# Attention and two expert layers on one core: sums in halves of banks, a second bank for the first products, idle products, and y stored by another queue

## The chip, the cores and the metric

The kernel runs on one core of one Trainium2 chip. A time is the device time of one execution in microseconds (us). Its parts are TensorE (PE, matrix products; its weight loads are listed as PEld), VectorE (DVE), ScalarE (ACT), GpSimd (POOL) and SyncE (SP); transfers are issued by SP's queue and by ACT's queue and are moved by 16 DMA engines.

## The reference

Three stages, one after the other, all in float32 at the interface:

```
state = alpha[t] * state + k[t] v[t]^T ;  y[t] = q[t] state     # 4 batches, 8 heads, 768 steps, head size 48
x = y as 3072 tokens x 384
out = sum over e of p[:, e] * (relu(x @ w1[e]) @ w2[e])         # 4 experts, 384 -> 1024 -> 384, p normalised
h = out @ w_in ; result = (h * clip(h + 3, 0, 6) / 6) @ w_out   # 384 -> 2048 -> 384; w_in, w_out arrive as float64
```

## The kernel before

**Attention** is done in 12 pieces of 256 time steps (n = 0 to 11; class `Attention`). A piece is a tree: products of q, k and alpha on DVE (`p0` to `p3`, `u0`, `u1`, `kk`, `kq`, `tp`), transposes on PE (`T_tp`, `T_k0` ... `T_q1`, copied out by ACT), four levels of score products (`Sc` copies by ACT, `C` products on PE, `Su` updates on DVE, level 0 to 3), `M` masks, `K` and `U` for the state, `Y`, `L` and `ST` summing y in two banks of PSUM, and `Z` for the running state. `A` copies y out of PSUM (tiles `ys0`, `ys1`, ACT) and stores it to DRAM (`x_d`) in four transfers; `R` loads it back with tokens in the order the expert layer wants (`rx`), and `XS` splits it into a high and a low part (`xh` on ACT, `xl` on DVE). `load_vt` fetches v again for `U` (`vt`) and for the four levels of `L` (`vl`, eight transfers).

**The expert layers** work on 6 blocks of 512 tokens, block 0 in two halves of 256. A step takes 128 hidden units: `mm1` (nine products into one bank `ph`), ACT makes `hh = relu(ph)`, DVE makes the rest `hl` from `ph` and `hh`, and `mm2` adds nine products (three for each of the three 128-row pieces m) into the sums `po`. In program order `mm2` of a step stands behind `mm1` of the next one. A run of steps with one expert is a visit; when it ends, `finish` multiplies the three sums by the expert's weights on DVE (`t`, `pb`), and they are stored to DRAM (`acc_d`). Phase 0 does the first 7 slices of 256 hidden units (14 steps) for each block or half block, phase 1 the other experts, phase 2 the last layer.

The order on each engine is written out by hand. Piece 0 of attention and the start of piece 1 stand ahead of the first step (the `u(...)` calls); after that, groups of pieces 1 to 11 are put between the steps of phase 0 (`group`, `rest`, the tables GROUP, BETWEEN and CHUNK): two pieces to a half of block 0, two to each later block. Every engine takes its instructions in this order, and each of SP's and ACT's transfers waits on one of eight counters, DMAHW0 to DMAHW7, which the transfers of both queues take in turn; a transfer waits for the one that had its counter before.

PSUM has eight banks: four for attention (`psa`), one for `ph` (`ps1`), three for `po` (`ps2`).

Of the kernel before, what the change touches and what calls it, by code (L numbers as in the profile page):

```python
# [21 lines left out]
class Attention:  # L22
# [268 lines left out]
    def tree(self, n):  # L291
# [24 lines left out]
        def T(src, tag, half):  # L316
            if half == 0:
                s[tag] = wk(tag, [P, 2, NP, P])
            pt = self.ps(f"p{tag}{half}_{n}")
            for i in range(4):  # L320
                pe.transpose(pt[:, P * i : P * i + P], src[:, 4 * half + i].rearrange("p h d -> p (h d)"), self.ident)  # L321
            out = s[tag].rearrange("p j r (c i) -> p j i c r", i=8)[:, :, 4 * half : 4 * half + 4]
            src_ = pt.rearrange("p (i j c r) -> p j i c r", i=4, j=2, r=NP)
            for j in range(2):
                nc.scalar.copy(out[:, j], src_[:, j])

# [158 lines left out]
        def A():  # L485
            for j in range(2):
                ys = wk(f"ys{j}", [P, NP, P])
                nc.scalar.copy(ys, s["py"][j])
                for h in range(2):
                    nc.scalar.dma_start(  # L490
                        self.y_d.rearrange("(r h e) t -> h e r t", r=NP, h=2)[h][:, :, n * U + P * j : n * U + P * j + P],
                        ys[64 * h : 64 * h + D],
                    )
# [45 lines left out]
def tile_gla__then__moe__then__moe2(  # L539
# [52 lines left out]
    ps1 = ctx.enter_context(tc.tile_pool(name="ps1", bufs=1, space=PSUM))  # L592
    ps2 = ctx.enter_context(tc.tile_pool(name="ps2", bufs=3, space=PSUM))
    psa = ctx.enter_context(tc.tile_pool(name="psa", bufs=4, space=PSUM))

    three = const.tile([P, 1], F32, name="three")
# [174 lines left out]
    def mm1(vi, f):  # L771
# [6 lines left out]
        cs = slice(vv["lo"], vv["lo"] + n)  # L778
        other = late and (vv["kind"] == 2 or f % 2)
        ph = (psa if other else ps1).tile([P, 512], F32, tag="psa" if other else "ps1", name=f"ph_{vi}_{f}")  # L780
        fs = slice(z * P, z * P + P)
# [29 lines left out]
    def mm2(vi, f):  # L811
# [6 lines left out]
        nt = KT if vv["kind"] == 1 else n // P  # L818
        if first:
            second = vv["phase"] == 1 and vi % 2  # L820
            pools = [(psa, "psa") if second else (ps2, "ps2") if m < 3 else (ps1, "ps1") for m in range(nt)]
            accs[vi] = [pool.tile([P, 512], F32, tag=tag, name=f"po_{vi}_{m}") for m, (pool, tag) in enumerate(pools)]
        for m in range(nt):
            ms = slice(m * P, m * P + P)
            for o, (w, h) in enumerate(((wh, hh), (wl, hh), (wh, hl))):
                fl = dict(start=(first and o == 0), stop=(last and o == 2))
                if vv["kind"] == 1:
                    pe.matmul(accs[vi][m][:, 0:n], w[:, z, ms], h[:, 0:n], **fl)  # L828
                else:
                    pe.matmul(accs[vi][m][:, 0:DM], h[:, ms], w[:, z, :], **fl)  # L830
            if last:
                finish(vi, m)

# [25 lines left out]
    def finish(vi, m):  # L859
# [4 lines left out]
        if vv["kind"] == 1:  # L864
# [6 lines left out]
            if vv["phase"] == 0:  # L871
                after(1, lambda: nc.sync.dma_start(acc_d[vv["e"]][:, m, t0 : t0 + n], t[:, 0:n]))
                return
# [26 lines left out]
    def u(names, n=0):  # L900
        at.run(n, names)
# [3 lines left out]

    u("p0 p1 p2 u0 u1 cp kk kq tp T_tp T_k0 T_k1 T_q0 T_q1 p3 r0")
    at.load(1, "qka")
# [3 lines left out]
    load_w(1, 2)  # L911
    u("tls Sc0 C0 Su0 Sc1 r1 y0 C1 Su1 Sc2 y1 M0 Su2 Sc3 r2 C2 Su3 C3")
    sw(0, 0)
    u("y2 M2 K0 K1 y3 y4 y5 U Y L0 L1 L2 L3 X Z0 Z1 Z2 Z3 ST")
    at.load(1, "v")
# [154 lines left out]
```

## Time and profile before

| | us |
|---|---|
| median of 3 runs (lowest to highest) | 1458.64 (1457.69 to 1460.36) |
| the profiled execution | 1465.24 |
| its span in the trace | 1463.4 |
| PE busy, DVE busy, ACT busy | 1379.1, 839.8, 464.1 |

The profiled execution is the one that the rows below come from. A row of the timeline gives the start, the length, engine, line, what is written and read, the shape, and in brackets how long the engine had been idle before it and what ended that. Of the 40 slices of the page each stands for 36.6 us; the first 14 or so hold phase 0 with attention.

### The profile page before, as it was taken

The numbers are of one execution on the slowest core, as the hardware profiler recorded it, in microseconds if no ns is written. First come the engines' busy times: TensorE is split into PE (matmuls) and PEld (weight loads), VectorE is DVE, ScalarE is ACT, GpSimd is POOL, SyncE is SP. The second block draws the span as 40 slices with busy tenths as digits, with TensorE's granted clock in tenths as the row PEclk, the third lists the DMA queues.
The fourth block names the chain that finished last, engine by engine and source line by source line (L and its number), as shares of the span: only waits on it lengthen the run. The fifth ranks groups of instructions, "written<-read, shape, count | busy, mean of one in ns | idle before, by whom it ended". The sixth has DMA issues, their size and how long they took to land.

```text
span 1463.4 us, 25889 instructions
## 1 busy us (share of the span) xinstructions
PE 1379.1 (94%) x10772; PEld 1178.0 (80%) x10772; DVE 839.8 (57%) x1505; ACT 464.1 (32%) x843; POOL 91.5 (6%) x125
## 2 busy tenths in 40 slices
PE   4588889999999999999999999999999999999998
PEld 4477878777877787888888888888889989998997
DVE  7877866766658527875757576725543333333332
ACT  3544443333333313311111111113333333333333
POOL 2000000000000001221212121200000000000000
PEclk9788999999999999999999999999999999999999
DMA  7454442434323226632424242314201010101000
GB/s 207 139 146 135 124 132 67 135 96 136 105 81 105 84 62 216 213 123 73 133 72 133 72 133 73 119 38 125 93 26 44 1 44 0 44 1 44 1 22 22
DMA packets 127748, 132.32 MB, mean 90 GB/s; under 512 B 33680, under 2 KB 109456, under 8 KB 127632
## 3 DMA queue, kind: packets, MB, share of 16 engines
q1 hardware_dynamic: 117648, 125.96, 28.3%
q10 hardware_dynamic: 9984, 4.72, 1.3%
q8 instruction: 84, 1.38, 0.4%
q14 instruction: 32, 0.26, 0.1%
HBM read 100.71 MB, written 34.65 MB: 92 GB/s over the span
## 4 chain that ended last, share of the span: by engine, by line
PE 85%; DMA 6%; DVE 5%; ACT 2%; issue 1%; SPq 1%; ACTq 0%; DVEq 0%
PE ph L785 39%; PE po L828 24%; PE po L830 13%; DMA vl<-vd 4%; PE py L455 2%; PE py L476 1%; PE pa L365 1%; DMA rw<-in_moe_w_dram 1%; PE pu L401 1%; PE pk L389 1%; PE pkt L321 1%; DVE kt L353 1%; PE pqt L321 1%; DMA x_d<-ys 1%; DVE hl L796 1%
## 5 line engine op out<-in xcount | busy, mean ns | idle before, releaser
L793 ACT ACTIVATE hh<-ph 128x512 fp32r<-128x512 f32 (+1 forms) x206 | 117.2, 569 | 539.1 <-PE ph L785 539.1
L785 PE MATMUL ph<-xh,w0h 128*128 128x512 f32 (+1 forms) x906 | 262.2, 399 | 24.5 <-DVE hl L796 22.5
L796 DVE SCALAR_TENSOR_TENSOR hl<-ph,hh 128x512 fp32r<-128x512 f32 (+1 forms) x206 | 134.3, 652 | 242.1 <-ACT hh L793 241.8
L785 PE MATMUL ph<-xh,w0l 128*128 128x512 f32 (+1 forms) x906 | 252.6, 388 | 0.0
L785 PE MATMUL ph<-xl,w0h 128*128 128x512 f32 (+1 forms) x906 | 252.2, 388 | 0.0
L828 PE MATMUL po<-hh,w1h 128*128 128x512 f32 (+1 forms) x618 | 236.1, 382 | 2.7 <-DVE t L870 2.5
L828 PE MATMUL po<-hh,w1l 128*128 128x512 f32 (+1 forms) x618 | 234.5, 379 | 0.0
L828 PE MATMUL po<-hl,w1h 128*128 128x512 f32 (+1 forms) x618 | 234.1, 379 | 0.0
L785 PEld LDWEIGHTS ph<-xh,w0h 128*128 128x128 f32 x906 | 165.2, 194 | 51.4 <-DVE hl L796 25.6
L785 PEld LDWEIGHTS ph<-xh,w0l 128*128 128x128 f32 x906 | 171.0, 194 | 35.1
L785 PEld LDWEIGHTS ph<-xl,w0h 128*128 128x128 f32 x906 | 171.1, 194 | 34.7
L804 DVE SCALAR_TENSOR_TENSOR g<-g,ph 128x512 f32<-128x512 f32 x96 | 66.0, 688 | 191.1 <-ACT g L801 191.1
L828 PEld LDWEIGHTS po<-hh,w1h 128*128 128x128 f32 x618 | 119.7, 194 | 25.8 <-issue 2.3
L828 PEld LDWEIGHTS po<-hh,w1l 128*128 128x128 f32 x618 | 119.6, 194 | 21.2
L828 PEld LDWEIGHTS po<-hl,w1h 128*128 128x128 f32 x618 | 118.9, 192 | 21.4
L830 PE MATMUL po<-w1h,hh 128*128 128x384 f32 x384 | 130.1, 339 | 1.8 <-ACT hh L805 1.7
L830 PE MATMUL po<-w1h,hl 128*128 128x384 f32 x384 | 129.8, 338 | 0.2
L830 PE MATMUL po<-w1l,hh 128*128 128x384 f32 x384 | 129.0, 336 | 0.0
L801 ACT ACTIVATE g<-ph,three 128x512 f32<-128x512 f32 x96 | 66.2, 690 | 178.2 <-PE ph L785 178.2
L806 DVE SCALAR_TENSOR_TENSOR hl<-g,hh 128x512 fp32r<-128x512 f32 x96 | 66.6, 693 | 67.0 <-ACT hh L805 67.0
L805 ACT ACTIVATE hh<-g 128x512 fp32r<-128x512 f32 x96 | 60.6, 632 | 76.1 <-DVE g L804 76.1
L830 PEld LDWEIGHTS po<-w1h,hh 128*128 128x128 f32 x384 | 72.2, 188 | 7.8 <-ACT hh L805 2.5
(102 smaller groups left out, 1399.1 us busy)
## 6 DMA issues: line engine op xcount, KB each, us to landing
rx<-x_d SPq DMA_DIRECT2D x36, 384.0 KB
rw<-in_moe_w_dram SPq DMA_DIRECT2D x28, 384.0 KB
vl<-vd SPq DMA_DIRECT2D x96, 96.0 KB
pb<-p_d SPq DMA_DIRECT2D x28, 256.0 KB
raw<-in_moe_w_in_dram SPq DMA_DIRECT2D x24, 256.0 KB
raw<-in_moe_w_out_dram SPq DMA_DIRECT2D x24, 256.0 KB
acc_d<-t SPq DMA_DIRECT2D x20, 256.0 KB
rq<-in_q_dram SPq DMA_DIRECT2D x24, 192.0 KB
```

The source lines that it names most:

```text
L321: pe.transpose(pt[:, P * i : P * i + P], src[:, 4 * half + i].rearrange("p h d -> p (h d)"), self.ident)
L353: tt(zv, zv, tlv[:, :, 1 - x].unsqueeze(2).to_broadcast([P, nb, w]), op=mul)
L455: pe.matmul(s["py"][j][64 * h : 64 * h + 64, r, :].rearrange("p (b x w) -> p b x w", x=2, w=w)[:, :, 1, :], self.vl[64 * j : 64 * j + 64, ...
L785: pe.matmul(ph[:, 0:n], w[:, j, fs], x[:, j, cs], start=(o == 0 and j == 0), stop=(o == 2 and j == KT - 1),)
L793: nc.scalar.activation(hh[:, 0:n], ph[:, 0:n], AF.Relu)
L796: nc.vector.scalar_tensor_tensor(hl[:, 0:n], ph[:, 0:n], 0.0, hh[:, 0:n].bitcast(F32), op0=ALU.max, op1=sub)
L801: nc.scalar.activation(g[:, 0:n], ph[:, 0:n], AF.Relu, bias=three)
L804: nc.vector.scalar_tensor_tensor(g[:, 0:n], g[:, 0:n], 6.0, ph[:, 0:n], op0=ALU.min, op1=mul)
L805: nc.scalar.activation(hh[:, 0:n], g[:, 0:n], AF.Copy, scale=1.0 / 6.0)
L806: nc.vector.scalar_tensor_tensor(hl[:, 0:n], g[:, 0:n], 1.0 / 6.0, hh[:, 0:n].bitcast(F32), op0=mul, op1=sub)
L828: pe.matmul(accs[vi][m][:, 0:n], w[:, z, ms], h[:, 0:n], **fl)
L830: pe.matmul(accs[vi][m][:, 0:DM], h[:, ms], w[:, z, :], **fl)
```

## The change

1. The four stores of y are issued by SP's queue (`nc.sync`) in place of ACT's, at the same place of the program; the stores of `acc_d` are put off by one step more (`after(2)`).
2. In the two halves of block 0 `ph` takes two banks in turn (`ps1`, `ps3`). The three sums of 256 columns share two banks (`psh`): m = 0 and 1 are the halves of one bank, m = 2 has the other. The sums 0 and 1 are finished together. From block 1 on the pools are as before.
3. In piece 0, `qt` is copied out of PSUM by DVE in place of ACT; `tls` stands between `T_q0` and `T_q1`, and `p3 r0` behind both. The first split of weights (`sw(0, 0)`) moves from the middle of piece 0 to its end.
4. A function `busy(n)` issues n products of the identity with itself into a bank that nobody reads: 30 ahead of piece 0, 6, 5, 5 and 5 inside it, 20 behind it.

```diff
-                nc.scalar.copy(out[:, j], src_[:, j])
+                if n == 0 and tag == "qt":
+                    nc.vector.tensor_copy(out[:, j], src_[:, j])
+                else:
+                    nc.scalar.copy(out[:, j], src_[:, j])
...
-                    nc.scalar.dma_start(
+                    nc.sync.dma_start(
                         self.y_d.rearrange(...)
...
-    ps2 = ctx.enter_context(tc.tile_pool(name="ps2", bufs=3, space=PSUM))
+    psh = ps_ctx.enter_context(tc.tile_pool(name="psh", bufs=2, space=PSUM))
+    ps3 = ps_ctx.enter_context(tc.tile_pool(name="ps3", bufs=1, space=PSUM))
+    ps2 = None
...
+        elif vv["n"] < NB and f % 2:
+            pool, tag = ps3, "ps3"
...
+        half = n < NB
+        if first and half:
+            po = [psh.tile([P, 2, U], F32, tag="psh", name=f"po_{vi}_{x}") for x in range(2)]
+            accs[vi] = [po[0][:, 0], po[0][:, 1], po[1][:, 0]]
...
-                fl = dict(start=(first and o == 0), stop=(last and o == 2))
+                fl = dict(start=(first and o == 0 and not (half and m == 1)), stop=(last and o == 2))
...
-            if last:
-                finish(vi, m)
+            if last and (m > 0 or not half):
+                for x in (0, 1) if half and m == 1 else (m,):
+                    finish(vi, x)
...
-                after(1, lambda: nc.sync.dma_start(acc_d[vv["e"]][:, m, t0 : t0 + n], t[:, 0:n]))
+                after(2, lambda: nc.sync.dma_start(acc_d[vv["e"]][:, m, t0 : t0 + n], t[:, 0:n]))
...
+    def busy(n):
+
+        for _ in range(n):
+            pe.matmul(idle[:, 0:P], at.ident, at.ident, start=True, stop=True)
...
-    u("p0 p1 p2 u0 u1 cp kk kq tp T_tp T_k0 T_k1 T_q0 T_q1 p3 r0")
+    busy(30)
+    u("p0 p1 p2 u0 u1 cp kk kq tp T_tp T_k0 T_k1")
+    u("T_q0 tls T_q1")
+    busy(6)
+    u("p3 r0")
...
-    u("tls Sc0 C0 Su0 Sc1 r1 y0 C1 Su1 Sc2 y1 M0 Su2 Sc3 r2 C2 Su3 C3")
-    sw(0, 0)
-    u("y2 M2 K0 K1 y3 y4 y5 U Y L0 L1 L2 L3 X Z0 Z1 Z2 Z3 ST")
+    u("Sc0 C0 Su0 Sc1 r1")
+    busy(5)
+    u("y0 C1 Su1 Sc2 y1")
+    busy(5)
+    u("M0 Su2 Sc3 r2 C2 Su3")
+    busy(5)
+    u("C3 y2 M2 K0 K1 y3 y4 y5 U Y L0 L1 L2 L3 X Z0 Z1 Z2 Z3 ST")
+    sw(0, 0)
+    busy(20)
```

The instructions of ACT around the stores of y of piece 4 (`ys_4`), in block 1, before; `kc_5` and `qc_5` are the copies of level 0 and 1 of piece 5:

```order
L343 COPY kc_5_2972<-kt_2830 128x512 [waits Activation_49]
L343 COPY qc_5_2974<-qt_2957 128x512 [waits Activation_49]
L793 ACTIVATE hh_1_2991<-ph_1_2981 128x512 [waits DVE_49,PE_49]
L488 COPY ys_4_2995<-py_4_2737 128x512 [waits DMAHW6_49,DMAHW4_49]
L490 DMA x_d<-ys_4_2995 48x4x128 [waits DMAHW5_49,Activation_49]
L490 DMA x_d<-ys_4_2995 48x4x128 [waits DMAHW7_49]
L488 COPY ys_4_2999<-py_4_2738 128x512 [waits DMAHW3_49,DMAHW1_49]
L490 DMA x_d<-ys_4_2999 48x4x128 [waits DMAHW2_49,Activation_49]
L490 DMA x_d<-ys_4_2999 48x4x128 [waits DMAHW4_49]
L343 COPY kc_5_3049<-kt_2830 128x512 [waits DVE_49,PE_49]
L343 COPY qc_5_3051<-qt_2957 128x512 [waits DVE_49]
L793 ACTIVATE hh_2_3065<-ph_2_3055 128x512 [waits PE_49]
```

and now:

```order
L346 COPY kc_5_3043<-kt_2901 128x512 [waits Activation_49]
L346 COPY qc_5_3045<-qt_3028 128x512 [waits Activation_49]
L804 ACTIVATE hh_1_3059<-ph_1_3049 128x512 [waits DVE_49,PE_49]
L491 COPY ys_4_3063<-py_4_2808 128x512 [waits DMAHW1_49,DMAHW0_49]
L491 COPY ys_4_3067<-py_4_2809 128x512 [waits DMAHW3_49]
L346 COPY kc_5_3122<-kt_2901 128x512 [waits DVE_49,PE_49]
L346 COPY qc_5_3124<-qt_3028 128x512 [waits DVE_49]
L804 ACTIVATE hh_2_3141<-ph_2_3131 128x512 [waits PE_49]
```

The four transfers with their waits for the counters have gone from between the copies and `kc_5`.

SP's queue at the same place before, from the stores of `acc_d` to the load of x (`rx_4`):

```order
L872 DMA acc_d<-pb_2038 128x256 [waits DMAHW5_49,DVE_49]
L124 DMA rv_3007<-in_v_dram 128x1x384 [waits DMAHW6_49]
L124 DMA rv_3007<-in_v_dram 128x1x384 [waits DMAHW7_49]
L145 DMA vt<-vd_2692 128x2x384 [waits DMAHW2_49,DMAHW0_49,PE_49]
L151 DMA vl<-vd_2692 64x1x384 [waits DMAHW1_49,PE_49]
L151 DMA vl<-vd_2692 64x1x384 [waits PE_49]
L151 DMA vl<-vd_2692 64x1x384 [waits DMAHW3_49,PE_49]
L151 DMA vl<-vd_2692 64x1x384 [waits DMAHW4_49,PE_49]
L151 DMA vl<-vd_2692 64x1x384 [waits DMAHW6_49]
L151 DMA vl<-vd_2692 64x1x384 [waits DMAHW0_49]
L151 DMA vl<-vd_2692 64x1x384 [waits DMAHW1_49]
L151 DMA vl<-vd_2692 64x1x384 [waits DMAHW3_49,PE_49]
```

and now, from the load `vd` that stands ahead:

```order
L137 DMA vd_2763<-in_v_dram 2048x1x48 [waits DMAHW2_49]
L493 DMA x_d<-ys_4_3063 48x4x128 [waits DMAHW3_49,Activation_49]
L493 DMA x_d<-ys_4_3063 48x4x128 [waits DMAHW4_49]
L493 DMA x_d<-ys_4_3067 48x4x128 [waits DMAHW5_49,Activation_49]
L493 DMA x_d<-ys_4_3067 48x4x128 [waits DMAHW6_49]
L124 DMA rv_3075<-in_v_dram 128x1x384 [waits DMAHW7_49,DVE_49]
L124 DMA rv_3075<-in_v_dram 128x1x384 [waits DMAHW0_49]
L145 DMA vt<-vd_2763 128x2x384 [waits DMAHW2_49,DMAHW1_49,PE_49]
L151 DMA vl<-vd_2763 64x1x384 [waits PE_49]
L151 DMA vl<-vd_2763 64x1x384 [waits DMAHW3_49,PE_49]
L151 DMA vl<-vd_2763 64x1x384 [waits DMAHW4_49,PE_49]
L151 DMA vl<-vd_2763 64x1x384 [waits DMAHW5_49,PE_49]
```

The stores of y stand at the head, ahead of the loads of v, `vt` and `vl`; the stores of `acc_d` have moved behind `vl`. Before, the counters that the eight loads `vl` skip are those of ACT's stores of y.

PE in block 0, a step of the visit that goes with piece 2, before (`ph_2` is the third `mm1` of the visit, `hh_1` and `hl_1` belong to the step before it):

```order
L785 MATMUL ph_2_1427<-xh_0_643,w0h_1098 128x256 [waits DVE_49]
L785 MATMUL ph_2_1427<-xh_0_643,w0h_1098 128x256 x2
L785 MATMUL ph_2_1427<-xh_0_643,w0l_1099 128x256 x3
L785 MATMUL ph_2_1427<-xl_0_644,w0h_1098 128x256 x3
L828 MATMUL po_0_1390<-hh_1_1381,w1h_956 128x256 [waits Activation_49]
L828 MATMUL po_0_1390<-hh_1_1381,w1l_957 128x256
L828 MATMUL po_0_1390<-hl_1_1382,w1h_956 128x256
L828 MATMUL po_1_1391<-hh_1_1381,w1h_956 128x256
```

and now:

```order
L796 MATMUL ph_2_1500<-xh_0_718,w0h_1172 128x256 x3
L796 MATMUL ph_2_1500<-xh_0_718,w0l_1173 128x256 x3
L796 MATMUL ph_2_1500<-xl_0_719,w0h_1172 128x256 x3
L849 MATMUL po_0_1461<-hh_1_1452,w1h_1030 128x256 [waits Activation_49]
L849 MATMUL po_0_1461<-hh_1_1452,w1l_1031 128x256
L849 MATMUL po_0_1461<-hl_1_1453,w1h_1030 128x256 [waits DVE_49]
L849 MATMUL po_0_1461<-hh_1_1452,w1h_1030 128x256
L849 MATMUL po_0_1461<-hh_1_1452,w1l_1031 128x256
```

The wait for DVE has moved from the first product of `mm1` to the third product of `mm2`, and the second three products of `mm2` go to the same tile as the first.

## Rows read from the trace of the kernel before

**Rows 1.** The page: busy time of the engines, share of the span, instructions.

```profile
PE 1379.1 (94%) x10772; PEld 1178.0 (80%) x10772; DVE 839.8 (57%) x1505; ACT 464.1 (32%) x843; POOL 91.5 (6%) x125
```

**Rows 2.** The busy table by stage: up to the first step, the first half of block 0, the second half, blocks 1 to 5 of phase 0 as far as attention reaches. Columns: from:to, length, busy time and instructions of PE, PEld, DVE, ACT, POOL, granted clock, DMA share, GB/s.

```profile
0.00:49.59 49.59, 20.65 (x420) 18.23 (x420) 39.03 (x78) 20.66 (x44) 10.04 (x29) 0.92 0.62 170
49.59:126.00 76.41, 59.62 (x941) 55.37 (x942) 61.12 (x117) 33.45 (x70) 0.00 (x0) 0.80 0.50 142
126.00:205.88 79.88, 68.84 (x1263) 63.78 (x1262) 64.63 (x138) 35.88 (x83) 0.00 (x0) 0.94 0.48 134
205.88:525.80 319.92, 301.16 (x3824) 243.27 (x3823) 200.67 (x376) 116.64 (x242) 0.00 (x0) 0.95 0.34 100
```

**Rows 3.** The same table for single pieces of attention from block 1 on, cut at the transposes of q (pieces 5, 10 and 11), and the sum over all seven.

```profile
205.88:253.89 48.01, 44.25 (x554) 35.74 (x554) 27.54 (x53) 17.20 (x36) 0.00 (x0) 0.93 0.35 98
...
441.12:483.67 42.55, 41.51 (x553) 33.69 (x554) 34.68 (x67) 17.18 (x36) 0.00 (x0) 1.00 0.33 93
483.67:525.80 42.13, 40.38 (x544) 32.59 (x543) 15.52 (x27) 13.54 (x26) 0.00 (x0) 1.00 0.24 71
sum 319.92, PE 301.16 PEld 243.27 DVE 200.67 ACT 116.64 POOL 0.00; mean PE 43.02 PEld 34.75 DVE 28.67 ACT 16.66 POOL 0.00
```

**Rows 4.** Who made PE wait from 205.88 to 525.8: total, times, longest.

```profile
PE pa L365 <- ACT qc L343: 14.3, 7, 3.2
PE ph L785 <- DVE hl L796: 4.4, 7, 0.7
```

**Rows 5.** PE's timeline at two products of level 1 and the `mm1` behind them, in the second half of block 0 and in piece 10.

```profile
146.56 1.13 PE L365 MATMUL pa<-qc,kc 48*64 48x64 f32 x32 [4.68 <-ACT qc L343]
...
451.49 0.69 PE L365 MATMUL pa<-qc,kc 48*64 48x64 f32 x32 [0.29 <-ACT qc L343]
452.90 0.96 PE L785 MATMUL ph<-xh,w0h 128*128 128x512 f32 x3 [0.71 <-DVE hl L796]
```

**Rows 6.** ACT's timeline in block 1 where piece 4's y is stored.

```profile
211.93 0.59 ACT L488 COPY ys<-py 128x512 f32<-128x512 f32 x1 [1.37 <-DMA rv<-in_v_dram]
214.51 3.33 ACTq L490 DMA_DIRECT2D x_d<-ys  x2
217.94 0.62 ACT L343 COPY kc<-kt 128x512 f32<-128x512 f32 x1 [5.43 <-DMA x_d<-ys]
```

**Rows 7.** The chain that ended last, at the same place (start, length, what), and where the loads `vl` end on SP's queue.

```profile
211.72 5.79 DMA vl<-vd
...
217.54 0.31 ACTq L490
...
217.94 0.63 ACT kc L343
...
220.54 4.21 PE ph L785 x9
...
228.23 2.27 PE ph L785 x9
```

**Rows 8.** SP's timeline there (the load of v and the eight loads `vl`), and PE's timeline at the first `L` of piece 5, which reads them.

```profile
206.94 1.19 SPq L124 DMA_DIRECT2D rv<-in_v_dram  x2
...
209.74 6.17 SPq L151 DMA_DIRECT2D vl<-vd  x8
...
239.96 1.16 PE L455 MATMUL py<-asb,vl 64*64 64x64 f32 x64
```

**Rows 9.** Who made PE wait in the first and in the second half of block 0.

```profile
PE ph L785 <- DVE hl L796: 14.8, 6, 5.8
...
PE pa L365 <- ACT qc L343: 1.5, 1, 1.5
...
PE pa L365 <- ACT qc L343: 6.8, 4, 4.7
PE ph L785 <- DVE hl L796: 3.3, 5, 1.7
```

**Rows 10.** ACT's and DVE's timeline in block 0: a cast of weights, and a copy and an update of level 1.

```profile
71.22 0.83 ACT L745 CAST w1h<-rw 128x768 fp32r<-128x768 f32 x1 [6.16 <-DMA rw<-in_moe_w_dram]
...
145.37 0.62 ACT L343 COPY kc<-kt 128x512 f32<-128x512 f32 x1 [4.89 <-DMA x_d<-ys]
...
146.02 0.69 DVE L353 TENSOR_TENSOR kt<-kt,tl 128x512 f32<-128x512 f32 x1 [4.76 <-ACT kc L343]
```

**Rows 11.** POOL, PE and DVE in piece 0 and up to the first step.

```profile
2.88 0.29 POOL masks.py:199 TENSOR_SCALAR_AFFINE_SELECT ident<-ident 128x128 f32<-128x128 f32 x1
...
12.66 0.66 PE L309 MATMUL ptt<-ident,tp 128*128 128x128 f32 x2 [12.66 <-DVE tp L232]
13.11 1.92 PE L321 MATMUL pkt<-ident,kp 128*128 128x128 f32 x8
...
49.59 1.01 PE L785 MATMUL ph<-xh,w0h 128*128 128x256 f32 x3 [1.96 <-ACT xh L764]
...
18.69 0.69 DVE L353 TENSOR_TENSOR kt<-kt,tl 128x512 f32<-128x512 f32 x1 [3.48 <-ACT kc L343]
...
27.96 0.95 DVE L746 TENSOR_TENSOR w0l<-rw,w0h 128x768 fp32r<-128x768 f32 x1
```

**Rows 12.** The chain that ended last, later in block 0: a `mm1`, and eight transposes.

```profile
111.20 2.29 PE ph L785 x9
...
119.75 1.02 PE pk L389 x8
```

More of the change, by code (lines that the diff above doesn't have):

```diff
@@ L592, in tile_gla__then__moe__then__moe2 @@
     ps1 = ctx.enter_context(tc.tile_pool(name="ps1", bufs=1, space=PSUM))
-    ps2 = ctx.enter_context(tc.tile_pool(name="ps2", bufs=3, space=PSUM))
     psa = ctx.enter_context(tc.tile_pool(name="psa", bufs=4, space=PSUM))
+    ps_ctx = ExitStack()
+    psh = ps_ctx.enter_context(tc.tile_pool(name="psh", bufs=2, space=PSUM))
+    ps3 = ps_ctx.enter_context(tc.tile_pool(name="ps3", bufs=1, space=PSUM))
+    ps2 = None
     three = const.tile([P, 1], F32, name="three")
@@ L778, in mm1 @@
         cs = slice(vv["lo"], vv["lo"] + n)
-        other = late and (vv["kind"] == 2 or f % 2)
-        ph = (psa if other else ps1).tile([P, 512], F32, tag="psa" if other else "ps1", name=f"ph_{vi}_{f}")
+        pool, tag = ps1, "ps1"
+        if late and (vv["kind"] == 2 or f % 2):
+            pool, tag = psa, "psa"
+        elif vv["n"] < NB and f % 2:
+            pool, tag = ps3, "ps3"
+        ph = pool.tile([P, 512], F32, tag=tag, name=f"ph_{vi}_{f}")
         fs = slice(z * P, z * P + P)
@@ L818, in mm2 @@
         nt = KT if vv["kind"] == 1 else n // P
-        if first:
+        half = n < NB
+        if first and half:
+            po = [psh.tile([P, 2, U], F32, tag="psh", name=f"po_{vi}_{x}") for x in range(2)]
+            accs[vi] = [po[0][:, 0], po[0][:, 1], po[1][:, 0]]
+        elif first:
+            nonlocal ps2
+            if ps2 is None:
+                ps_ctx.close()
+                ps2 = ctx.enter_context(tc.tile_pool(name="ps2", bufs=3, space=PSUM, reuse_waits="tile"))
             second = vv["phase"] == 1 and vi % 2
@@ L825, in mm2 @@
             for o, (w, h) in enumerate(((wh, hh), (wl, hh), (wh, hl))):
-                fl = dict(start=(first and o == 0), stop=(last and o == 2))
+                fl = dict(start=(first and o == 0 and not (half and m == 1)), stop=(last and o == 2))
+                if half:
+                    fl["skip_group_check"] = True
                 if vv["kind"] == 1:
@@ L904, in sw @@
         split_w(y, i, nc.vector)
-    u("p0 p1 p2 u0 u1 cp kk kq tp T_tp T_k0 T_k1 T_q0 T_q1 p3 r0")
+    idle = ps1.tile([P, 512], F32, tag="ps1", name="idle")
+    def busy(n):
[6 more added lines that the diff above has]
+    u("p3 r0")
     at.load(1, "qka")
```

## The prediction

> **What bounds the kernel now.** I read the page first: PE is busy for 94% of the span [rows 1], so a gain can come only from the remaining time of PE and from stretches at the lower of its two clocks. The busy table by stage says where these are [rows 2]. After 525.8 us PE is all but full and nothing is changed there. Before it the span loses in four stages: PE is busy 20.65 of 49.59 us up to the first step, 59.62 of 76.41 in the first half of block 0, 68.84 of 79.88 in the second, 301.16 of 319.92 in the blocks behind, and the granted clock is 0.80 to 0.95 in the last three. Then the lists of waits, stage by stage, and the timeline around the longest waits.
>
> In the blocks behind (seven pieces of attention, 205.88 to 525.8) there are only two waits on PE, seven times each: for the copies of q at level 1, 14.3 us, and for `hl`, 4.4 us [rows 4]. ACT's timeline shows why: between the two copies of level 0 and of level 1 it stores y, and the copy `kc` behind the stores starts after 5.43 us of waiting for a transfer [rows 6]. The chain is plainer still: a load `vl` of SP's queue takes 5.79 us to land, then ACT issues a store in 0.31 us, then `kc` runs [rows 7]. In the order the stores wait for counters that the loads of v and `vl` had just taken, so ACT, and with it PE, waits for loads with which neither has to do. After such a wait nine products of `mm1` take 4.21 us where they take 2.27 a step later [rows 7], which is the half clock.
>
> **The stores of y.** Four transfers leave ACT at each piece. What stands behind `ys` on ACT is then the copy `kc` at once. For the blocks behind, the price is read from the pieces: piece 10 (441.12 to 483.67) shows what one costs almost without the jam, clock 1.00 and PE busy 41.51 of 42.55 us; piece 11 has 40.38 of 42.13 [rows 3]. Six at 41.51 and one at 40.38 are 289.4 us; the seven took 319.9 [rows 3], so 30.5 us are to be had. I take 28: piece 10 keeps 0.71 us of waiting for `hl` [rows 5], and about half of that in each piece may stay.
>
> What the stores cost on SP: each waits for its copy, and behind it stand the loads of v, `vt`, `vl`, then the stores of `acc_d` and the load of x. In block 1 the second copy of y, freed of the 1.37 us before it [rows 6], would end near 211.2; SP began its loads of v at 206.94, so it starts some 4 us later, and after four issues (3.33 us for two of them on ACT with its waits, 0.31 us for one without [rows 6, 7], so 1.2 to 6.7 us; I take 2.5) the loads of v start at 213.7 in place of 206.94. Everything behind moves by 6.8 us: `vl` is issued up to 222.7 in place of 215.9 [rows 8], and with the longest landing seen, 5.79, is there by 228.5. The first `L` runs at 239.96 now [rows 8] and would run 5.5 us earlier (the average of a piece's gain plus a little), at 234.5. So 6 us of cover are left in a block of 512 tokens, and I cost the move at nothing there. In block 0 a piece has half the steps to hide it; if the cover goes, PE waits at `L`, up to those few us per piece, and that is in the lower bounds below. The stores of `acc_d`, one step later and behind `vl`, free buffers that are needed a visit later; nothing.
>
> By the Trainium skill ("DMA: Bandwidth & Descriptors", section "Issuing engines are not separate DMA queues") starting transfers from several engines saves only the sequencer's time to start them, and transfers of all queues share the same engines. By that rule this part would be worth a few tenths of a microsecond per piece, since nothing about the transfers themselves changes; the row with the wait of 5.43 us speaks against applying it here, because what is waited for is not the store's own transfer. It is the second rival below.
>
> **Second half of block 0** (79.88 us). PE waits 6.8 us for the copies of q and 3.3 for `hl` [rows 9]. The longest, 4.68 us [rows 5], is the same jam: `kc` had waited 4.89 us on a store of y, and DVE's update stood idle for 4.76 [rows 10]. I take 6 of the 6.8 for the stores. The second bank lets `mm1` run while DVE still works on the `hl` of the step before, so that only `mm2` waits for it, behind another `mm1`; 2 of the 3.3. Together 8. The other end is DVE: it is busy 64.63 of the 79.88 [rows 2], so not over 15.2; the lower end is 3, if the loads behind the stores come late for `L`.
>
> **First half of block 0** (76.41 us). Here 14.8 us of waiting are put down to `hl` [rows 9], but the longest is not the bank's: ACT waited 6.16 us for weights to land before the cast at 71.22 [rows 10], and its relu stands behind that cast. Two banks let one `mm1` go ahead in such a gap, 2.29 us at the clock seen there [rows 12], twice or so, and the stores' part is the one wait of 1.5 [rows 9] with the slow products behind it. DVE is busy 61.12 [rows 2], the weights land no earlier. I take 5, bounds 0 and 15.3. That the sums of 256 columns share banks costs a wait for one more `finish` at three changes of visit, under a microsecond each; nothing.
>
> **Up to the first step** (49.59 us). The transposes at 13.11 run at half clock, 1.92 us for eight where eight take 1.02 later [rows 11, 12]. The 30 idle products can start when POOL has the identity, at 3.2 [rows 11]. No row shows one; a plain float32 product leaves two records where a transpose leaves one, so I estimate one at two transposes, 0.48 us or, at full clock, 0.26 [from rows 11, 12]. Thirty end between 10.9 and 17.6; the first transpose is ready at 12.66 [rows 11], so they cost up to 4.9 us or nothing. If the clock rises on the way, they end about when that is ready: nothing. DVE idles 3.48 us before 18.69 for ACT's copies [rows 11]; now it makes half of these copies itself (some 0.5 us each, 2 us), takes `p3 r0` behind them (1.9), and loses the split of weights (0.95, at 27.96 [rows 11]), so that it ends piece 0 up to half a microsecond earlier. Behind it PE's `Y`, `L` and `ST` at full clock save about 2, and DVE's start of piece 1 follows by 1; the first `mm1` is then not far behind ACT's `xh` [rows 11], perhaps at full clock. I take 2.5, bounds -4.9 and 6.
>
> **Sum.** 28 + 8 + 5 + 2.5 = 43.5 us against the profiled execution of 1465.2, which is 1421.7; the median of the runs stands 6.6 below that execution, so 1415. With all lower bounds (20 for the blocks behind if a third returns as other waits) the gain is 18, 1441; with all upper ones 67, 1392.
>
> **Rivals.** (1) *The wait moves.* ACT is free, but PE meets DVE's `hl` or the loads instead, and the blocks behind give back half, 14 us: 1429 to 1431. For it: piece 10 still has a wait on `hl`. Against: DVE is busy 28.67 of 45.7 us in a mean piece, with room [rows 3]. (2) *The stores are not what is waited for*; the transfers share the engines and the jam stays in another form. Only banks and start help: 2 + 4 + 2.5, about 8.5: 1450. Against it stands the chain with its 0.31 us issue. (3) *SP's head is blocked, and the kernel is slower.* The stores of y hold the loads `vl` past `L`. The cover is 6 us; from there each microsecond counts for each of eleven pieces, and the gain of 43.5 is used up at 4 us beyond it, so the loads would have to come 17 us later than now (6.8 + 6 + 4); at 19 the time is 1458.6 + 22 = 1480. The loads of v move by 6.8 by the sum above, so this needs another wait ahead of them. (4) *More*: block 0 comes near DVE's bound, and the gain passes 55: below 1403.
>
> **Numbers.** Forecast 0.66, with its own range 1403 to 1426; rival 1 0.19; rival 2 0.06; rival 3 (or idle products that run long, with the loads late) 0.04; rival 4 0.05. Runs of this kernel tell about 0.2% from no change, 3 us. Rival 2 lies beyond that on the fast side, so faster 0.94, same 0.02, slower 0.04. The range 1403 to 1438 leaves out rivals 2 to 4, some 0.15, and a little of rival 1.
>
> **What would show it.** In the changed profile ACT should have no `DMA_DIRECT2D` row, `kc` no wait for a transfer, PE no wait for `qc` over 0.5 us after block 0, the clock 1.00 in each piece behind, and a piece 41.5 to 42 us long. `mm1` in block 0 should wait for weights alone, and DVE should fill that stage. The first `mm1` should start near 47. Wrong I am if PE shows waits of `L` or `U` for `vl` or `vt`, if the pieces stay at 45 us or more, or if the first transpose starts well after 12.7.

## The result and the profile after

| | before | after |
|---|---|---|
| median (lowest to highest), us | 1459.5 (1457.69 to 1462.2), 4 runs | 1419.65 (1417.91 to 1421.36), 4 runs |
| the profiled execution, its span | 1465.24, 1463.4 | 1419.27, 1417.5 |

The ratio is 0.9725 (95% interval 0.9705 to 0.9746): 39.9 us between the medians, where 43.6 were forecast (1415 against 1458.6), and 45.9 between the two spans. The page after, busy time of PE and the granted clock in 40 slices, beside [rows 1]:

```profile
PE 1374.3 (97%) x10914; PEld 1175.8 (83%) x10914; DVE 840.0 (59%) x1509; ACT 460.9 (33%) x839; POOL 91.4 (6%) x125
...
PEclk9889999999999999999999999999999999999999
```

The busy table by stage, with the columns of [rows 2] and cut at the same places in the program:

```profile
0.00:47.33 47.33, 33.82 (x563) 31.13 (x563) 40.31 (x80) 18.50 (x40) 9.91 (x29) 0.96 0.65 177
47.33:120.38 73.05, 57.36 (x941) 52.20 (x942) 60.82 (x119) 33.20 (x70) 0.00 (x0) 0.84 0.51 148
120.38:191.44 71.06, 66.60 (x1263) 61.57 (x1262) 64.24 (x139) 35.32 (x83) 0.00 (x0) 0.98 0.55 152
191.44:479.41 287.97, 287.70 (x3823) 233.77 (x3823) 200.18 (x376) 116.70 (x242) 0.00 (x0) 1.00 0.39 111
```

Against [rows 2] the stages give 2.26, 3.36, 8.82 and 31.95 us, together 46.4; the rest of the program takes 0.5 us longer than before, which leaves 45.9. In the blocks behind, PE is now busy for 287.70 of 287.97 us and the clock is 1.00. Single pieces there, beside [rows 3]:

```profile
191.44:232.73 41.29, 41.29 (x553) 33.69 (x554) 27.45 (x53) 17.20 (x36) 0.00 (x0) 1.00 0.41 113
...
315.14:356.76 41.62, 41.51 (x555) 33.69 (x554) 33.43 (x64) 17.19 (x36) 0.00 (x0) 1.00 0.43 122
...
sum 287.97, PE 287.70 PEld 233.77 DVE 200.18 ACT 116.70 POOL 0.00; mean PE 41.10 PEld 33.40 DVE 28.60 ACT 16.67 POOL 0.00
```

Every piece lies between 40.25 and 41.62 us, and the list of PE's waits for this stretch, which had two lines before [rows 4], is empty. The timeline shows what became of the place where ACT stored y [rows 6, 8]; here ACT, then SP, then PE at the first `L` of piece 5:

```profile
195.51 1.09 ACT L491 COPY ys<-py 128x512 f32<-128x512 f32 x2
197.27 0.62 ACT L346 COPY kc<-kt 128x512 f32<-128x512 f32 x1 [0.67 <-PE pa L368]
...
196.14 1.83 SPq L493 DMA_DIRECT2D x_d<-ys  x4
198.06 1.20 SPq L124 DMA_DIRECT2D rv<-in_v_dram  x2
...
199.94 4.98 SPq L151 DMA_DIRECT2D vl<-vd  x8
...
218.80 1.16 PE L458 MATMUL py<-asb,vl 64*64 64x64 f32 x64
```

`kc` follows the two copies of y and waits 0.67 us for a product; the four stores take SP 1.83 us, and `vl` is issued up to 204.92, long before the `L` at 218.80.

In block 0 the waits are not gone but renamed. PE's list for the first half, then for the second, beside [rows 9]:

```profile
PE po L849 <- DVE t L892: 5.4, 1, 5.4
PE po L849 <- ACT hh L804: 4.5, 2, 4.0
PE po L849 <- DVE hl L807: 4.1, 4, 1.9
...
PE pa L368 <- ACT qc L346: 1.4, 2, 0.8
...
PE po L849 <- DVE t L892: 1.8, 1, 1.8
PE po L849 <- DVE hl L807: 1.2, 1, 1.2
PE pa L368 <- ACT qc L346: 1.1, 2, 0.6
```

`mm1` no longer waits for `hl` (14.8 us in the first half before), but `mm2` waits 14.0 us, for `t`, `hh` and `hl`. Behind the two longest of these waits stand two loads of weights. SP, ACT, DVE and PE in order:

```profile
56.58 5.37 SPq L151 DMA_DIRECT2D vl<-vd  x8
62.06 0.38 SPq L740 DMA_DIRECT2D rw<-in_moe_w_dram  x1
...
85.91 3.72 SPq L740 DMA_DIRECT2D rw<-in_moe_w_dram  x1
...
69.67 0.83 ACT L752 CAST w1h<-rw 128x768 fp32r<-128x768 f32 x1 [7.97 <-DMA rw<-in_moe_w_dram]
...
92.83 0.83 ACT L752 CAST w1h<-rw 128x768 fp32r<-128x768 f32 x1 [4.46 <-DMA rw<-in_moe_w_dram]
...
70.53 0.96 DVE L753 TENSOR_TENSOR w1l<-rw,w1h 128x768 fp32r<-128x768 f32 x1 [3.25 <-ACT w1h L752]
...
93.70 0.96 DVE L753 TENSOR_TENSOR w1l<-rw,w1h 128x768 fp32r<-128x768 f32 x1 [6.86 <-ACT w1h L752]
...
103.41 0.75 DVE L892 TENSOR_TENSOR t<-po,pb 128x256 f32<-128x256 f32 x2
...
70.84 0.58 PE L849 MATMUL po<-hh,w1h 128*128 128x256 f32 x1 [3.99 <-ACT hh L804]
...
104.30 0.55 PE L849 MATMUL po<-hh,w1h 128*128 128x256 f32 x1 [5.40 <-DVE t L892]
```

SP issues the load of w2 of slice 3 behind the eight loads `vl`, at 62.06. ACT waits for it 7.97 us, DVE behind ACT 3.25, and PE 3.99. The next time (issue 85.91, ACT 4.46, DVE 6.86) DVE comes so late that it reaches `t`, which frees the banks of the sums, at 103.41, and PE has waited 5.40 us. DVE's idle time behind the split of weights (3.25 and 6.86, together 10.1 us) is not new. This is its line in the kernel before, from the first product to piece 3:

```profile
DVE w1l L746 <- ACT w1h L745: 10.0, 3, 5.4
```

The change left this cause where it was.

### The profile page after: what moved, and what is told of

Its sections match the earlier page's. It is cut to its first block, busy times and chain, and to the rows that moved or that the text cites. A ratio compares the mean times of both kernels' runs of the same rounds, so it can differ in the third digit from the quotient of the medians.

```text
span 1417.5 us, 26167 instructions
## 1 busy us (share of the span) xinstructions
PE 1374.3 (97%) x10914; PEld 1175.8 (83%) x10914; DVE 840.0 (59%) x1509; ACT 460.9 (33%) x839; POOL 91.4 (6%) x125
## 2 busy tenths in 40 slices
DMA packets 127749, 132.33 MB, mean 93 GB/s; under 512 B 33680, under 2 KB 109456, under 8 KB 127632
## 4 chain that ended last, share of the span: by engine, by line
PE 89%; DVE 7%; DMA 1%; ACT 1%; issue 1%; SPq 0%; DVEq 0%; ACTq 0%
PE ph L796 41%; PE po L849 26%; PE po L851 14%; PE py L458 2%; PE pa L368 1%; PE py L479 1%; DMA rw<-in_moe_w_dram 1%; PE pu L404 1%; PE pk L392 1%; PE pkt L321 1%; PE pqt L321 1%; DVE qt L356 1%; DVE hl L807 1%; DVE dg L247 1%; PE py L442 1%
## 5 line engine op out<-in xcount | busy, mean ns | idle before, releaser
L796 PE MATMUL ph<-xh,w0h 128*128 128x512 f32 (+1 forms) x906 | 257.2, 393 | 2.7 <-ACT xh L771 2.4
L796 PE MATMUL ph<-xh,w0l 128*128 128x512 f32 (+1 forms) x906 | 248.4, 383 | 0.0
L796 PE MATMUL ph<-xl,w0h 128*128 128x512 f32 (+1 forms) x906 | 247.8, 382 | 0.3 <-DVE xl L772 0.3
L849 PE MATMUL po<-hh,w1h 128*128 128x512 f32 (+1 forms) x618 | 233.2, 377 | 14.1 <-DVE t L892 7.2
L796 PEld LDWEIGHTS ph<-xh,w0l 128*128 128x128 f32 x906 | 167.9, 190 | 34.3
L796 PEld LDWEIGHTS ph<-xl,w0h 128*128 128x128 f32 x906 | 167.4, 189 | 34.4 <-DVE xl L772 0.6
L796 PEld LDWEIGHTS ph<-xh,w0h 128*128 128x128 f32 x906 | 162.2, 190 | 27.8 <-ACT xh L771 2.6
```

The source lines that it names most:

```text
L796: pe.matmul(ph[:, 0:n], w[:, j, fs], x[:, j, cs], start=(o == 0 and j == 0), stop=(o == 2 and j == KT - 1),)
```

## The experiments

All profiles in one table, cut at PE's transposes of q, which stand in each build: first product of block 0; from there to the transposes of piece 3; on to those of piece 5 (the end of block 0, nearly); the six pieces 5 to 10; the rest of the span.

| build | first product | to piece 3 | to piece 5 | six pieces | rest |
|---|---|---|---|---|---|
| before | 49.59 | 84.91 | 71.31 | 277.79 | 979.80 |
| before, again (`b_again`) | 49.97 | 85.72 | 69.12 | 272.36 | 979.73 |
| stores alone (`y_on_sp`) | 49.91 | 82.08 | 63.70 | 247.74 | 978.17 |
| loads of v later (`v_loads_later`) | 49.59 | 81.07 | 66.73 | 247.73 | 978.18 |
| banks alone (`banks_only`) | 50.15 | 82.70 | 67.80 | 274.36 | 979.19 |
| start alone (`start_only`) | 47.98 | 86.10 | 69.90 | 276.25 | 980.57 |
| after | 47.33 | 81.55 | 62.49 | 247.73 | 978.40 |
| after, again (`a_again`) | 50.58 | 80.24 | 62.50 | 247.71 | 978.37 |
| after, y on ACT (`y_on_act`) | 50.50 | 82.00 | 67.77 | 265.80 | 978.63 |
| after, no idle products (`no_idle`) | 51.34 | 79.92 | 62.50 | 247.70 | 978.44 |
| after, last 20 left out (`no_last_idle`) | 48.30 | 79.53 | 62.94 | 247.71 | 979.92 |
| after, weights earlier (`w_ahead`) | 47.75 | 76.66 | 62.53 | 247.75 | 979.71 |
| the same, finish first (`w_ahead_finish`) | 47.91 | 74.79 | 63.18 | 247.76 | 978.46 |

A row is one execution. Those of `y_on_sp` and `v_loads_later` ran 3.1 and 4.1 us under the medians of their builds, so their rows are that much better than the typical run.

**The stores alone.** The kernel before with

```
-                    nc.scalar.dma_start(
+                    nc.sync.dma_start(
                         self.y_d...[h][:, :, n * U + P * j : n * U + P * j + P],
```

> The kernel before with one edit alone: y is stored by SP's queue. Theory of the prediction: ACT was held by its own stores, which waited for the completion of SP's loads; the store on SP takes that hold away, so the seven pieces fall from 45.70 to 41.2 to 41.6 us each, ACT has no wait for a transfer at kc, and the time is 1424 to 1431 us (1459.5 less 28 to 32, and up to 4 more in the second half of block 0, where one chunk's stores lie). Rival: the loads and stores share the engines that move the data, and whoever issues them the jam stays: the pieces stay over 44 us, the wait shows up at another instruction, and the time is 1450 or more.

Measured: 1426.5 us (1423.44 to 1427.68) beside 1457.29 for the kernel before, ratio 0.9787 (0.9772 to 0.9802). The six pieces fall to the length that they have in the changed kernel, to 0.01 us. ACT's list of waits from 195 to 490 us has no line for a transfer; what `kc` waits for is PE:

```profile
ACT kc L343 <- PE pa L365: 34.4, 21, 2.2
```

Three quarters of the whole gain is this edit: 31 us of medians. The rival, 1450 or more, is out.

**The same part undone.** The changed kernel with that word turned back.

> The changed kernel with y stored by ACT's queue again, all else of the change kept. Theory of the prediction: most of the 28 to 32 us of the blocks behind come back, 1444 to 1452 us, with waits of ACT for a transfer at kc. A finer form of it: each DMA of SP and ACT takes one of eight completion counters in turn, and a store on ACT waits until the transfer that held its counter last has landed; in this build the counters of the stores are mixed with those of the loads of vl in some pieces and not in others, so pieces alternate between about 41.5 us and 45 to 47, and the time lies at the low end. Rival (the transfers share engines, the queue does not matter): 1417 to 1424, pieces near 41.3.

Measured: 1445.2 us (1443.19 to 1446.66), ratio 0.9914 (0.9897 to 0.993); 18.1 us of the six pieces come back, and ACT waits for transfers again. A long and a short piece by the busy table, and ACT at the longest wait:

```profile
334.07:380.96 46.89, 44.31 (x557) 35.74 (x553) 33.61 (x64) 17.18 (x36) 0.00 (x0) 0.93 0.41 121
380.96:423.17 42.21, 41.04 (x540) 33.22 (x537) 27.20 (x52) 17.17 (x36) 0.00 (x0) 1.00 0.37 106
...
254.59 0.62 ACT L346 COPY kc<-kt 128x512 f32<-128x512 f32 x1 [4.97 <-DMA vl<-vd]
```

The time is where it was expected, at the low end. The pieces are indeed of two kinds, 42.2 to 42.9 and 45.1 to 46.9, but not in turn (42.89, 45.78, 45.13, 46.89, 42.21, 42.90), so the alternation that was expected did not come. Which counters are mixed in the order does not by itself say which piece is long; that it also hangs on when the transfers land is likely, but not shown.

**The stores kept on ACT, the loads moved.** This tells what ACT waits for. The kernel before with

```
-        if k == 1:
+        if k == 3:
             self.load(n + 1, "v")
             self.load_vt(n)
```

> The kernel before with one edit alone, and y still stored by ACT: the loads of v, vt and vl are issued two rests later (about 13 us), so that the four stores of y stand together in the order of the program, with no load of vl between them. If ACT was held by the landing of the loads that stood between its stores, the waits at kc go though the stores stay on ACT: pieces of 41.3 to 42 us, 1424 to 1433 us; a product that reads vt or vl late may give a little of it back. If a store on ACT costs ACT that time by itself (the issue, or the transfer of y), the waits at kc stay at 5 to 6 us a piece and the time at 1450 to 1460.

Measured: 1429.28 us (1425.14 to 1429.61), ratio 0.9803 (0.9787 to 0.9818). ACT's list of waits from block 1 on has no line for a transfer. At the place of [rows 6], and a piece of the busy table:

```profile
202.17 0.81 ACTq L490 DMA_DIRECT2D x_d<-ys  x2
...
203.69 0.80 ACTq L490 DMA_DIRECT2D x_d<-ys  x2
204.59 0.62 ACT L343 COPY kc<-kt 128x512 f32<-128x512 f32 x1 [0.93 <-DVE dg L247]
...
197.39:238.66 41.27, 41.27 (x556) 33.69 (x552) 27.45 (x53) 17.20 (x36) 0.00 (x0) 1.00 0.41 114
```

ACT still issues all four stores, two in 0.8 us, and `kc` comes 0.93 us behind them in place of 5.43. So neither the issue of a store nor the queue was the cost; ACT waited for loads that stood between its stores and had not landed. That the link between them is the completion counter that a store takes over from a load is read from the order of the built program; no row of a trace names a counter. The pieces are as long as with the stores on SP. Only the stretch to piece 5 is 3.0 us longer: PE waits for copies of q 2.2 us there in place of 1.1, and part of it runs at a granted clock of 0.95 in place of 1.00.

**Where the first profile's 6.6 us lay.** The kernel before once more.

> The kernel before, unchanged, profiled a second time. The profiled execution shown of it took 1465.24 us, 6.6 over the median of its runs, and that of the changed kernel 1419.27, at its own median of 1419.65. First theory: the 6.6 us lay in the waits that the change removed (the six stores of y, whose length hangs on when transfers land): then this second profile differs from the first in the seven pieces behind block 0 (319.92 us together) and hardly elsewhere; with a time near 1459 the seven pieces sum to about 314. Second theory: the 6.6 us are spread over the whole program or lie at its ends: then the pieces keep 319 to 321 us whatever the time.

Measured: 1458.73 us, 6.5 less. The six pieces take 272.36 us, 5.4 less, and the stretch to piece 5 another 2.2 less, while the first two are 1.2 longer. The first theory holds in the main, as far as two executions tell: most of what differs between them is the length of the jams. Piece 8 took 47.64 us in the first profile and 43.66 in the second; piece 5 is much as it was [rows 3]:

```profile
204.81:252.03 47.22, 43.02 (x556) 34.82 (x553) 27.55 (x53) 17.20 (x36) 0.00 (x0) 0.96 0.35 99
...
344.56:388.22 43.66, 41.55 (x557) 33.69 (x553) 33.52 (x64) 17.18 (x36) 0.00 (x0) 1.00 0.40 118
```

**The banks alone.** The kernel before with the diff's parts on `psh`, `ps3`, `half`.

> The kernel before with the banks alone: two banks for the first products of block 0 and its sums in halves of banks; stores of y on ACT, start as before. The changed kernel lies some 9 us under the one with the stores alone (ratios 0.9725 and 0.9787 to the kernel before), so banks and start share about 9. First theory (the prediction's): a second bank lets mm1 run while hl is still late, 2 us in each half of block 0, against a wait for one more finish: 1452 to 1456 where the kernel before is at 1457 to 1459, a ratio of 0.997 to 0.999. Rival: the half banks cost as much as the second bank gains (the wait of 5.40 us for t at the first change of visit), ratio 0.999 to 1.002, and the 9 us come from the start.

Measured: 1455.37 us (1450.0 to 1460.77, 12 runs), ratio 0.9974 (0.9961 to 0.9987): about 3.8 us gained, the size that the first theory had. PE's waits from the first product to piece 3 show the same exchange as in the changed kernel:

```profile
PE po L846 <- DVE t L889: 5.4, 1, 5.4
PE po L846 <- ACT hh L801: 4.2, 2, 3.9
PE po L846 <- DVE hl L804: 4.0, 4, 1.9
```

13.6 us at `mm2` stand for the 14.8 at `mm1`. The bank lets PE run ahead of DVE, and then PE waits for DVE anyway, for nearly as long.

**The start alone.** The kernel before with the order, the copies on DVE and the 61 idle products.

> The kernel before with the start alone: half of piece 0's copies on DVE, the new order, the 61 idle products; banks and stores as before. First theory: the first product of block 0 starts 2 to 2.5 us earlier (47.3 in place of 49.6) and no more than that comes of it, a ratio of 0.998 to 0.9995. Rival: the higher clock and the order gain more behind the first product, 5 to 7 us, ratio 0.995 to 0.9965.

Measured: 1461.25 us (1457.31 to 1462.73, 12 runs), ratio 1.0012 (1.0 to 1.0024). Neither theory: the first product comes 1.6 to 2 us earlier, and the next stage is 0.4 to 1.2 us longer (its waits for `hl` are 15.7 us, not 14.8 [rows 9]); by the timing nothing is gained.

So banks and start, each by itself, do not make up the 9 us that they were thought to share: the three ratios (0.9787, 0.9974, 1.0012) multiply to 0.9773, against 0.9725 for the changed kernel, and some 7 of its 40 us come only when the parts are together. The next runs say which part that is: stores and banks multiply to 0.9761, and the changed kernel without its idle products has 0.9754. By these ratios, whose intervals are some 0.2% to either side, most of it is the idle products, which gain in the changed kernel what they do not gain in the kernel before. The stores of `acc_d`, a step later in the change, were not run by themselves.

**The idle products.** The changed kernel without all 61 (the lines `busy(...)`), and without the last 20.

> The changed kernel without any of the idle products, its order and copies kept. If the idle products raise the clock of piece 0, the first product of block 0 starts 1 to 2 us later than 47.33 and the time is 1 to 3 us over the changed kernel, a ratio of 0.973 to 0.975 to the kernel before. Rival: the products cost PE as much as the clock gives back (30 of them ran 8.49 us and ended 0.45 us before the first transpose; 20 behind ST ran 6.36 us): the same ratio as the changed kernel, 0.971 to 0.973, with the first product within 0.5 us of 47.33.

> The changed kernel without the 20 idle products behind ST, the other 41 kept. Without all 61 the first product of block 0 came at 51.34 in place of 47.33, and the time rose by about 3 us. If the gain lies in the copies and products of piece 0 before ST (half-clock rows of 1.92 us that take 1.04 with the idle products), the 20 bring under a microsecond, by the 8 transposes of k behind them alone: first product of block 0 near 48.2, time 0 to 1 us over the changed kernel. If most of the gain lies in the clock with which block 0 begins, its first piece is 1 to 2 us longer too, and the time 1.5 to 3 us over it.

> The changed kernel, unchanged, beside the next two on one chip: a ratio of 0.9705 to 0.9746 to the kernel before, as the first timing had it, and the stages of its first profile within 1 us.

Measured: without any 1423.02 us (1421.04 to 1424.91), ratio 0.9754 (0.9734 to 0.9773); without the last 20 1420.64 (1418.02 to 1421.03), 0.9731 (0.9715 to 0.9746); the changed kernel again 1418.84 (1417.78 to 1421.39), 0.9719 (0.9705 to 0.9734). The 61 together are worth some 4 us by the medians, though the first and the last interval just touch; the last 20 no difference that these runs tell. Without the 61 the first product comes at 51.34, 4.0 us later where 1 to 2 were expected, and later than in any build with the old start (49.59 to 50.15): in that profile the new order and DVE's copies by themselves are a loss. The second profile of the changed kernel was a surprise, as its stages were expected within 1 us of the first: its first product came at 50.58, not 47.33. The same products at level 0 and 1 of piece 0 in the first profile and in the second, with the idle products between them, and the busy table of both for 18 to 29 and 29 to 37 us:

```profile
18.25 1.38 PE L933 MATMUL idle<-ident 128*128 128x128 f32 x10
20.54 0.69 PE L368 MATMUL pa<-qc,kc 48*64 48x64 f32 x32 [0.90 <-ACT qc L346]
...
18.79 2.35 PE L933 MATMUL idle<-ident 128*128 128x128 f32 x10
21.07 1.13 PE L368 MATMUL pa<-qc,kc 48*64 48x64 f32 x32
```

```profile
18.00:29.00 11.00, 7.50 (x158) 6.38 (x148) 10.97 (x19) 4.39 (x8) 0.00 (x0) 1.00 0.78 236
29.00:37.00 8.00, 6.57 (x258) 5.78 (x259) 6.71 (x15) 2.63 (x7) 0.00 (x0) 1.00 0.64 159
...
18.00:29.00 11.00, 9.27 (x166) 8.12 (x166) 10.96 (x19) 3.97 (x8) 0.00 (x0) 0.84 0.83 253
29.00:37.00 8.00, 7.01 (x216) 6.52 (x217) 5.24 (x13) 1.17 (x5) 0.00 (x0) 0.57 0.58 137
```

The five idle products took 2.35 us there in place of 1.38, in a stretch with a granted clock of 0.84 on the mean; the next has 0.57. So what the start gains depends on the execution. Of the seven profiles with all or most of the idle products the first product lies between 47.33 and 48.30 in five, and at 50.50 and 50.58 in two, both with 0.84 and 0.57. The second stretch is what sets them apart: `no_last_idle` has 0.84 and then 1.00, `w_ahead` 0.69 and then 1.00, and their first products come at 48.30 and 47.75. Why the clock fell there is open. Of the 3.25 us that the second profile starts later, 1.3 are made up by piece 3 (its transposes come at 130.82 against 128.88; in `no_idle` at 131.26), and 1.9 are left at the end. So `no_idle` is 2.4 us behind the first profile at piece 3, but only 0.4 behind the second: the 4 us are a figure of the medians, and no pair of profiles shows all of it.

**Weights earlier, a better version.** The changed kernel with

```
     load_w(0, 3)
+    load_w(1, 3)
...
-            nxt = (1, i) if y == 0 else (0, i + 1)
+            nxt = (y, i + 1)
```

and, in the second build, `mm2` with its `finish` ahead of the rest of the piece at a visit's last step:

```
+            ahead = done and visits[done[0]]["n"] < NB and done[1] == len(visits[done[0]]["steps"]) - 1
+            if ahead:
+                mm2(*done)
             if rest:
                 at.rest(rest.pop(0))
...
-            if done:
+            if done and not ahead:
                 mm2(*done)
```

> The changed kernel with the loads of weights in block 0 issued one split earlier (the load of w2 of a slice no longer behind the loads of q, k, a, v for the next piece on SP). In the changed profile ACT waits 7.97 and 4.46 us for two of them, DVE idles 3.25 and 6.86 us behind, and PE then waits 3.99 us for hh and 5.40 for t. First theory: DVE, busy 60.5 of the 72.7 us from the first product to 120.04, is what the first half of block 0 waits for, and the 10.1 us of its idle time are to be had in large part: 5 to 9 us under the changed kernel, a ratio of 0.966 to 0.969 to the kernel before. Rival: the wait moves (to the copies of q, to hl, or to the loads that now come later), 0 to 2 us, ratio 0.971 to 0.9725.

> The changed kernel with the weights' loads earlier, as in the run before, and at the last step of a visit in block 0 the second products and finish ahead of the two reductions of the next piece on DVE (1.9 us). With the loads alone PE still waits 2.71 us for t at the first change of visit. If that wait is DVE's order, up to 1.9 us of it goes at each of three changes of visit, and the time is 1 to 4 us under that of the earlier loads alone (ratio 0.967 to 0.969). If DVE is full anyway, what is put off is late in its turn: same time, ratio 0.969 to 0.971, with a longer wait for the next copies of q.

Measured: 1415.25 us (1412.37 to 1417.31), ratio 0.9699 (0.9679 to 0.9719), and 1413.46 (1412.77 to 1414.11), 0.9685 (0.9671 to 0.9699). The second lies under the changed kernel beside it (1418.84) by 5.4 us, and its interval ends below; the first is about 4 under and its interval overlaps. The rows of `w_ahead` on DVE, and PE's waits in `w_ahead_finish` from the first product to piece 3:

```profile
59.44 0.96 DVE L190 TENSOR_TENSOR w<-rq,rk 128x768 f32<-128x768 f32 x1 [1.29 <-DMA rk<-in_k_dram]
...
89.05 0.96 DVE L753 TENSOR_TENSOR w1l<-rw,w1h 128x768 fp32r<-128x768 f32 x1 [3.37 <-DMA rw<-in_moe_w_dram]
```

```profile
PE po L849 <- DVE hl L807: 7.3, 5, 3.4
...
PE po L849 <- DVE t L892: 0.9, 1, 0.9
```

DVE's 10.1 us of idle time behind the weights shrink to 3.7, with 1.3 new for `rk`, whose load now goes behind theirs. The wait for `t` falls from 5.4 to 2.7 and then 0.9; that for `hl` rises from 4.1 to 7.3. DVE is busy for 68.56 of 74.79 us there: it nearly fills this stage now. The first theory had the mechanism; the loads alone gave a little less than its 5 to 9 us, both edits together its lower end. Whether two of the loads could come earlier still was not tried.

## Why the prediction was right

The mechanism held for the stores, which are most of the gain, and the likeliest case came: forecast 1415, own range 1403 to 1426, measured 1419.65. What was expected of the banks and of the start held in part, and errors of both signs met in the sum. Term by term, against the profiled executions:

- **"I take 28" for the stores in the blocks behind**: 31.95 measured, over the 30.5 that "are to be had". Two sizes were off. Of the 0.71 us for `hl` "about half of that in each piece may stay": nothing stayed, with the stores alone neither. And "six at 41.51" took PE's busy time of piece 10 for all six; they measure 40.84 to 41.62, on the mean 41.29. The price also hangs on the execution it was read from: the six pieces give 30.1 us against the first profile of the kernel before and 24.6 against the second (277.79 and 272.36 less 247.73).
- **SP's side, "I cost the move at nothing"**: right. The loads of v start 6.69 us after the piece's transposes of q (191.37 to 198.06), 1.13 before (205.81 to 206.94 [rows 8]), so 5.6 later against 6.8 forecast; `vl` is out 3.5 later, its eight issues having taken 4.98 in place of 6.17 us; the first `L` comes 27.43 us after the transposes in place of 34.15, 6.7 earlier against 5.5. PE waits for no load.
- **Second half of block 0, "Together 8"**: 8.82. The stores alone bring the stretch to piece 5 from 71.31 or 69.12 to 63.70, so 5.4 to 7.6 us ("6 of the 6.8"); banks and start take another 1.2 ("2 of the 3.3").
- **First half, "I take 5"**: 3.36, over-sized. The stores alone give 2.8 to 3.6 here, where "the one wait of 1.5" with the slow products behind it was their part. Banks and start on top of them give about 0.5 in the first profile and 1.8 in the second. By themselves the banks give 2.2 to 3.0 and the start loses 0.4 to 1.2: against the first profile of the kernel before the three parts sum to 3.9, and the changed kernel has 3.4 and 4.7 less, so they add up as far as single profiles tell. The step that failed here is "two banks let one `mm1` go ahead in such a gap, 2.29 us at the clock seen there, twice or so": it does, but the time is waited for at `mm2`, because DVE, not PE, is late.
- **"A wait for one more `finish` ... under a microsecond each; nothing"**: at the first change of visit the wait is 5.40 us. Most of it is the lateness of DVE's order: 2.71 and 0.90 remain when DVE is early. What the shared banks cost by themselves was not tried.
- **"I take 2.5" up to the first step**: 2.26 in the first profile, but a loss of 1.0 in the second, which ends 1.9 us later all told; that the first came so close is luck. By itself the start gives nothing (ratio 1.0012), and its new order and copies without the idle products show a loss (51.34 in one profile), where the sum had DVE done "up to half a microsecond earlier". The estimate that thirty idle products end "about when that is ready" was right: 11.71 and 12.16, and 12.80 and 12.71 the second time.
- **"The median of the runs stands 6.6 below that execution, so 1415"**: this step of the sum failed. By the second profile the 6.6 us lay mainly in the jams themselves, so they were counted twice: once within the 43.5 and once as the distance to the median. The profiled execution after, 1419.27, stands at its own median. 1421.7 less the 2.5 by which the sum was short is 1419.2.

Of the rivals, "the wait moves" holds for block 0 alone, where 14.8 us at `mm1` became 14.0 at `mm2`; the blocks behind gave nothing back: PE's list of waits is empty there. The second, with the rule of the Trainium skill ("DMA: Bandwidth & Descriptors", section "Issuing engines are not separate DMA queues") that transfers of all queues share the same engines, would have left pieces of 45 us. No run here speaks against the rule: the bytes moved are the same (132.32 MB before, 132.33 after). What changed is which engine waits for the transfers, and of that the rule does not speak. The third needed loads 17 us later; they came 5.6 later.

Of the signs, these came as written: no DMA row on ACT, `kc` free of transfers, clock 1.00, pieces of "41.5 to 42 us" (even shorter). "The first `mm1` should start near 47" came in the first profile (47.33) and not in the second (50.58). Two did not come. "`mm1` in block 0 should wait for weights alone": it waits for `xh` and `xl` at the start, 2.4 and 0.3 us, and it is `mm2` that waits for DVE and for weights. "DVE should fill that stage": it is busy 60.82 of 73.05 us, because it waits 10.1 us behind weights.

## What to carry to other kernels

The stores on ACT's queue cost ACT little by their issue (two in 0.8 us) and much by their wait (5.43 us at one place). With stores on a computing engine's queue, look in the order of the program for what else takes the same completion counters, and keep loads with long landings from standing between such stores, or let an idle queue issue them. Where PE waits for a late engine, another bank may do little but move the wait to the next product (here 14.8 us became 13.6); look for what makes that engine late. A part that gains nothing by itself can gain once another jam is gone, so time it both ways. And where a jam is what varies between executions, take the gain and the base from the same execution, and do not subtract the distance to the median again.

## What was not expected of the hardware

The half pace of PE's products at the start is not in the column of the granted clock. In the kernel before, the eight transposes at 13.11 take 1.92 us [rows 11], and in the changed kernel 1.04 at 12.44, while the column reads 1.00 for both between 3.2 and 18 us. From 18 to 37 us it reads 0.55 in `banks_only` and 1.00 in the kernel before, yet PE is busy for 12.90 and 12.91 us there, and the first row of score products (`pa`) takes 1.13 and 1.14. The pace of a product of known shape was the better sign. The Trainium skill ("TensorE: Matmul & The Clock Gate", section "Seeing it yourself") warns that a trace's records of the clock have been seen to be unreliable; these rows agree. Also, the granted clock in the first 50 us differs between executions of one program (0.84 and 0.57 against 1.00 and 1.00 above). In these two the first products lie 3.25 us apart, but the ends only 1.9.
